# Paced loads, reordered weight sums and a split last product in a fused attention and MLP kernel on one Trainium2 core

## The chip, the cores and the metric

The kernel runs on one core of one Trainium2 chip. The metric is the device time of one execution in microseconds (us); the median of several executions is given, with the lowest and the highest. A profile is taken from one more execution, whose own time is given beside it. The engines are called by their short names: PE (matrix products; PEld is its loading of weights), DVE and ACT (elementwise work), POOL (which here issues most loads), SP (which issues stores and transposes).

## The reference

Two stages follow each other. The first is linear attention with a decay `lam` per head, over 4 batches, 8 heads, 768 positions and 64 channels. In blocks of positions, with a running state S of 64 x 64 per head:

```
out_block = ((q k^T) * decay_mask) v  +  (q * lam^(pos+1)) S
S         = lam^block * S  +  (k * lam^(block-1-pos))^T v
```

The second takes the attention output as x, 3072 tokens by 512, and is a two-layer network:

```
h = x @ w_in                       # 512 -> 2048
g = h * tanh(log(1 + exp(h)))      # Mish
out = g @ w_out                    # 2048 -> 512
```

Inputs and the output are float32; the kernel computes its products in float16 with float32 sums.

## The kernel before

**Tiles and groups.** The sequence is cut into chunks of 128 positions. Chunk i = 4 n + b is piece n of batch b, and the four chunks of one n make a group of 512 tokens; there are six groups, n = 0 to 5. The network of group n runs on PE while attention of the next groups is worked in between its units.

**Loads.** POOL issues nearly all loads (they turn float32 into float16 on the way): K, Q and V of each chunk (`load_k`, `load_q`, `load_v`, L61 to L78), the weight w_in in six tiles whose column bounds stand in `cuts` (L82), and w_out in four tiles of 512 rows (L98). In program order the first group's chunks come first, then w_in, w_out, then the second group's chunks 4 to 7. The list `ahead` (L314) holds the twelve loads of the third group, chunks 8 to 11: K and Q of each chunk in turn, then the four V. The loop over the first group's units takes two of them after each unit from 25 to 29 (L645), and the last two go out after the first unit of group 1 (L684). Later groups' loads go out one by one behind `pace()` (L395), a copy of one element on POOL that waits for the newest entry of the list `mark`, an output of Mish or of a copy on ACT.

**Attention.** For chunks 0 to 7 the `look_...` functions are used: `look_t` (L204) transposes K and Q on PE, evicts K's transpose on ACT (pkT) and Q's on DVE (pqT); `look_s` (L226) makes the scores, masked on DVE; `look_kv` the state's increment; `look_o` the output. `scale_k` (L262) makes the decayed K (ktil), on DVE but for chunks 6 and 7, which POOL makes. From chunk 8 on `turn` (L269) scales K and lets two DMA transposes, issued on SP, make qraw and kraw; pairs of chunks are then worked by `pair_s` (scores, L338), `pair_o` and `pair_a`. In group 1 the turns of chunks 8, 9, 10 and 11 are issued after units 0, 1, 4 and 7, and `pair_s` of chunks 8 and 9 stands after unit 11.

**The network.** Units 0 to 15 are w_in products with Mish on ACT behind each. The second product is done with seven products instead of eight on halves of g and w_out: P1, P5, P6, P2, P7, P3, P4 (`fast_unit`, L550). They need sums of quarters of w_out, `tsum` 0 to 3, made once on DVE by `weight_sum(i, s)` (L452), in two halves s; half s = 1 of every sum but 0 needs the last w_out tile. They also need sums of quarters of g, `gsum` (`token_sum`, L465). P6 reads sum 1, P5 sum 0, P7 sum 2 and P4 sum 3. In group 0 the units are numbered 16, 17 (P1), 18, 19 (P5), 20 to 23 (P6, P2, P6, P2, in halves of the inner dimension), 24, 25 (P7), 26, 27 (P3), 28, 29 (P4). A loop (L625 to L649) runs these units and puts in between what the dictionaries name: weight sums after units 14, 15, 18 and 20, ktil of chunk 4 after unit 22, `look_t(4)` after 23, `look_s(4)` after 24, and so on.

**What follows a product.** `after(n, step)` (L526) copies a finished PSUM bank into the next product's bank or into an SBUF tile, and issues the store. P1's bank x is copied to z, to which P6 adds; P6's z is copied to y, P7 and then P4 add to z, P3 adds to y. P7 and P3 get P5's product added on DVE (`plus`, L518). The last P4 of the last group (L561) is done in three pieces: block 0 whole, block 1 in two halves of 128 columns; each is copied by ACT from bank z and stored from SP.

**Order.** The program is scheduled by hand: each engine and each queue works in the order in which the instructions are written. Waits are put in by data, PSUM bank and buffer.

Of the kernel before, what the change touches and what calls it, by code (L numbers as in the profile page):

```python
# [20 lines left out]
def kernel(  # L21
# [10 lines left out]
    nc = tc.nc  # L32
# [46 lines left out]

    WS = 4  # L80

    cuts = (0, 128, 256, 512, 1024, 1536, DF)  # L82
    win = [const.tile([128, NKC, b_ - a_], F16, name=f"win{a_}") for a_, b_ in zip(cuts, cuts[1:])]

    def w_in(ni, kc):
# [309 lines left out]
    def pace():  # L395
        nc.gpsimd.tensor_copy(paced, mark[-1])  # L396
# [125 lines left out]
        store(n, r, c, o, nc.sync)  # L522

    p5 = {}

    def after(n, step):  # L526

        if step == "P1":
            nc.scalar.activation(places(n, "z"), bank[n, "x"], AF.Copy)
        elif step == "P2":  # L530
            o = work.tile([128, 2, HN], F32, name="osum", tag="osb", bufs=4)
            nc.scalar.activation(o, bank[n, "x"], AF.Copy)
            mark.append(o[0:1, 0, 0:1])
            store(n, 0, 0, o, nc.scalar)
        elif step == "P6":
            nc.scalar.activation(places(n, "y"), bank[n, "z"], AF.Copy)
        elif step == "P5":
            p5[n] = work.tile([128, 2, HN], F32, name="p5", tag="p5", bufs=1)
            nc.scalar.activation(p5[n], bank[n, "w"], AF.Copy)
            mark.append(p5[n][0:1, 0, 0:1])  # L540
        elif step == "P7":
            plus(n, 1, 1, "z")
        elif step == "P3":
            plus(n, 0, 1, "y")
        elif step == "P4":
            o = work.tile([128, 2, HN], F32, name="osum", tag="osb", bufs=4)
            nc.scalar.activation(o, bank[n, "z"], AF.Copy)  # L547
            store(n, 1, 0, o, nc.scalar)

    def fast_unit(n, step, blk, part=None):  # L550

        key, lhs, rhs = {
            "P1": lambda: ("x", g_quarter(n, 0, 0), w_part(0, 0)),
            "P2": lambda: ("x", g_quarter(n, 0, 1), w_part(1, 0)),
            "P6": lambda: ("z", g_sum(n, 1), w_sum(1)),
            "P5": lambda: ("w", g_sum(n, 0), w_sum(0)),
            "P7": lambda: ("z", g_sum(n, 2), w_sum(2)),
            "P3": lambda: ("y", g_sum(n, 3), w_part(1, 1)),
            "P4": lambda: ("z", g_quarter(n, 1, 1), w_sum(3)),
        }[step]()  # L560
        if n == NG - 1 and step == "P4":  # L561
            for lo, hi in ((0, HN),) if blk == 0 else ((0, HN // 2), (HN // 2, HN)):
                product(n, key, lhs, rhs, False, blk, None, lo, hi)
                o = work.tile([128, 1, HN], F32, name="osum", tag="osb", bufs=4)
                nc.scalar.activation(o[:, 0, lo:hi], bank[n, "z"][:, blk, lo:hi], AF.Copy)  # L565
                store(n, 1, 0, o[:, :, lo:hi], nc.sync, blk, lo, hi)
            return
        for b in range(2) if blk is None else (blk,):
            product(n, key, lhs, rhs, step in ("P1", "P5"), b, part)
        if blk != 0 and part != 0:  # L570
            after(n, step)

    nc.scalar.activation(lbh, lnb, AF.Exp, scale=float(C))
    nc.scalar.activation(lk, lnb, AF.Exp, scale=ek)
# [48 lines left out]
    units += [(fast_unit, (0, step, blk)) for step in ("P7", "P3", "P4") for blk in range(2)]  # L623
    sums = {3: ((2, 0),), 7: ((2, 1),), 11: ((0, 0), (1, 0), (3, 0)), 15: ((0, 1), (1, 1)), 16: ((3, 1),)}
    for u, (fn, args) in enumerate(units):  # L625
        fn(*args)
        if 8 <= u < 8 + NVB - B:
            nc.vector.memset(vz[u - 8 + B][:, :, D : 2 * D], 0.0)
        elif u == 13:
            nc.vector.tensor_scalar(out=maskT, in0=rel, scalar1=0.0, scalar2=None, op0=ALU.is_ge)  # L630
        for i, s in {14: ((0, 0),), 15: ((0, 1),), 18: ((1, 0), (2, 0), (3, 0)),
                     20: ((1, 1), (2, 1), (3, 1))}.get(u, ()):
            weight_sum(i, s)
        for i, part in sums.get(u, ()):
            token_sum(0, i, part)
        if u == 22:
            scale_k(4)
        then = [f(i, "po" if i == 5 else "ph") if f is look_kv else f(i) for f, i in visit.get(u, ())]
        if u == 23:
            scale_k(5)  # L640
            scale_k(6)
        for f in then:
            if f:
                f()
        if u >= 25:  # L645
            for _ in range(2):
                ahead.pop(0)()
        if u == 26:
            scale_k(7)  # L649
    next_state(1, 0)  # L650

    for n in range(1, NG):
        r, s, t = Pair(), Pair(), Pair()
        r.n, r.bs, s.n, s.bs, t.n, t.bs = n, (2, 3), n + 1, (0, 1), n + 1, (2, 3)
        visit = {}
        if n > 1:
            visit[0] = pair_o, last
        if 1 < n < NG - 1:
            visit[5] = pair_a, r
        if n < NG - 1:  # L660
            visit[9 if n > 1 else 11] = pair_s, s
            visit[16] = pair_o, s
            visit[26] = pair_s, t
        if n < NG - 2:
            visit[21] = pair_a, s
        last = t
        turns = {23: (n + 2) * B, 25: (n + 2) * B + 1}
        turns.update({1: 9, 4: 10, 7: 11} if n == 1 else {3: (n + 1) * B + 2, 6: (n + 1) * B + 3})
        units = [(mm1_duo, (n, g, lo, lo + GT // 2)) for lo in (0, GT // 2) for g in range(NKI // 2)]
        steps = ("P1", "P5", "P6", "P2", "P7", "P3", "P4")  # L670
        units += [(fast_unit, (n, step, blk)) for step in steps for blk in range(2)]
        later = []
        if n < NG - 2:
            later = [(lambda f=f, i=(n + 2) * B + b: f(i)) for f, b in (
                (load_k, 0), (load_q, 0), (load_k, 1), (load_q, 1), (load_k, 2), (load_q, 2),
                (load_v, 0), (load_v, 1), (load_k, 3), (load_q, 3), (load_v, 2), (load_v, 3))]
        sums = {9: ((2, 0),), 11: ((2, 1),), NKI - 3: ((0, 0), (1, 0)), NKI - 1: ((0, 1), (1, 1)),
                NKI + 4: ((3, 0),), NKI + 5: ((3, 1),)}
        for u, (fn, args) in enumerate(units):
            fn(*args)  # L680
            if n == 1 and u == 0:
                turn(8)
                look_s(7)
                while ahead:  # L684
                    ahead.pop(0)()
            if n == 1 and u == 2:
                f = look_kv(7)
                look_o(7)
                f()
                next_state(1, 1)  # L690
            if later and (8 <= u < 16 or u in (17, 19, 21, 23)):
                pace()
                later.pop(0)()
            for i, part in sums.get(u, ()):
                token_sum(n, i, part)
            if turns.get(u, NG * B) < NG * B:
                turn(turns[u])
            if u in visit:
                f, s_ = visit[u]
                s_.spare = ("po", "po") if u < NKI - 1 else ("pS", "pk") if f is pair_a else ("ph", "po")  # L700
                f(s_)
# [30 lines left out]
```

## Time and profile before

| | us |
|---|---|
| median of 3 executions | 204.13 |
| lowest and highest | 204.04 and 205.29 |
| the profiled execution, its own time | 205.4 |
| span of the profiled execution, first to last instruction | 203.6 |
| chain that ended last: share of PE | 71% |
| chain that ended last: share of DMA | 17% |

In the profile, a row of the timeline or of the chain gives start, duration and what was done, with the idle time of the engine ahead of it and what ended that in square brackets. L434 is line 434 of the kernel. A row of the table of waits gives who waited for whom, the sum, the number of times and the longest. A row of a group of instructions gives line, engine, operation, output and inputs with shapes, the count, then busy time and the mean of one in ns, then idle time before them. All times are in us from the start of the span.

### The profile page before, as it was taken

Reading aid. Unit: us, or ns where it says so; the run is one execution under the profiler, and the core shown is the slowest. Engines: PE = TensorE matmul, PEld = TensorE weight load, DVE = VectorE, ACT = ScalarE, POOL = GpSimd, SP = SyncE. Lnnn points to the kernel's source line nnn. Section 1 sums busy time; section 2 is a strip of 40 time slices with the busy share of each in tenths; the row PEclk is TensorE's granted clock in tenths of the full one; section 3 lists DMA queues with packets and bytes.
Section 4 is the critical chain, followed back from the end, with each engine's and each line's share of the span. In section 5 each row is a group of like instructions: output and inputs, shape, how many; then the busy total and the mean of one; then the engine's idle time right before and its main releaser. Section 6 shows DMA issues by size and latency. Waiting matters only on the chain.

```text
span 203.6 us, 5043 instructions
## 1 busy us (share of the span) xinstructions
PE 192.7 (95%) x2080; PEld 160.3 (79%) x2080; DVE 131.1 (64%) x248; ACT 91.9 (45%) x160; POOL 81.0 (40%) x124
## 2 busy tenths in 40 slices
PE   7869999899997999999999999999999999999992
PEld 3554447678885998998998998998988988988881
DVE  7897169689943878847878757878557817215420
ACT  5784664233664431365531455420565330666311
POOL 7997333589907583005992006982000000000000
PEclk9999999999999999999999999999999999999999
DMA  9999999999999999956999989999981023500033
GB/s 132 140 156 183 201 206 199 153 193 183 177 148 129 154 119 193 225 123 76 103 127 182 221 131 88 96 98 187 276 110 29 0 55 103 159 0 0 3 103 103
DMA packets 112985, 26.81 MB, mean 132 GB/s; under 512 B 102594, under 2 KB 112962, under 8 KB 112962
## 3 DMA queue, kind: packets, MB, share of 16 engines
q0 software_dynamic: 78080, 13.37, 91.4%
q1 hardware_dynamic: 30848, 9.97, 29.1%
q10 hardware_dynamic: 4034, 3.15, 5.0%
q8 instruction: 16, 0.26, 0.5%
q14 instruction: 7, 0.06, 0.1%
HBM read 27.26 MB, written 6.29 MB: 165 GB/s over the span
## 4 chain that ended last, share of the span: by engine, by line
PE 71%; DMA 17%; POOL 5%; DVE 3%; ACT 1%; issue 1%; ACTq 0%; POOLq 0%
PE ph L434 29%; PE z L494 15%; DMA wout<-in_moe_w_out_dram 10%; PE x L494 9%; PE y L494 5%; DMA kraw<-ktil 4%; PE w L494 4%; DMA win<-in_moe_w_in_dram 3%; PE pS L349 2%; PE pO L376 2%; POOL vz L78 2%; POOL kn L67 1%; PE pv L328 1%; POOL qn L75 1%; PE pO L357 1%
## 5 line engine op out<-in xcount | busy, mean ns | idle before, releaser
L434 PE MATMUL ph<-xt,win 128*128 128x256 f16 x640 | 73.0, 273 | 0.0
L434 PEld LDWEIGHTS <-win 128*128 128x128 f16 x640 | 61.6, 98 | 7.5 <-issue 0.3
L441 ACT ACTIVATE hsg<-ph 128x512 f16<-128x512 f32 x80 | 47.8, 597 | 30.7 <-PE ph L434 30.7
L494 PEld LDWEIGHTS <-gsum 128*128 128x128 f16 x384 | 36.9, 98 | 6.0 <-issue 1.2
L480 DVE TENSOR_TENSOR gsum<-hsg 128x1024 f16<-128x1024 f16 x24 | 16.6, 691 | 29.6 <-ACT hsg L441 22.4
L494 PEld LDWEIGHTS <-hsg 128*128 128x128 f16 x296 | 27.9, 98 | 4.4 <-issue 1.1
L494 PE MATMUL z<-tsum,gsum 128*128 128x256 f16 x192 | 23.3, 273 | 1.0 <-DVE tsum L461 1.0
L494 PE MATMUL x<-wout,hsg 128*128 128x256 f16 x192 | 23.7, 273 | 0.0
L67 POOL DMA_DIRECT2D kn<-in_k_dram x23 | 20.6, 894 | 7.5 <-DMA win<-in_moe_w_in_dram 2.6
L75 POOL DMA_DIRECT2D qn<-in_q_dram x23 | 20.4, 889 | 5.9 <-DMA wout<-in_moe_w_out_dram 4.3
L78 POOL DMA_DIRECT2D vz<-in_v_dram x24 | 21.2, 891 | 4.0 <-DMA wout<-in_moe_w_out_dram 1.7
L396 POOL COPY paced<-hsg 1x1 f16<-1x1 f16 x27 | 8.7, 324 | 35.1 <-ACT hsg L441 35.1
L365 DVE TENSOR_TENSOR sb<-pS,maskT 128x512 f16<-128x512 f32 x32 | 19.9, 684 | 1.9 <-PE pS L349 1.6
L288 DVE TENSOR_TENSOR raw<-pv,state 64x256 f32<-64x256 f32 x24 | 10.1, 422 | 12.8 <-PE pv L328 12.5
L265 DVE TENSOR_TENSOR ktil<-kn,lk 128x512 f16<-128x512 f16 (+1 forms) x22 | 14.9, 684 | 0.0
L405 PE MATMUL ph<-xt,win 128*128 128x512 f16 x64 | 14.2, 379 | 0.3 <-DMA win<-in_moe_w_in_dram 0.3
L384 DVE TENSOR_TENSOR xtok<-pO,lqt 128x256 f16<-128x256 f32 x32 | 11.3, 416 | 3.9 <-PE pO L376 3.9
L547 ACT ACTIVATE osum<-z 128x512 f32<-128x512 f32 x5 | 3.0, 597 | 23.6 <-PE z L494 23.6
L494 PE MATMUL z<-tsum,hsg 128*128 128x256 f16 (+1 forms) x104 | 12.0, 264 | 0.8 <-ACT osum L565 0.8
L405 PEld LDWEIGHTS <-win 128*128 128x128 f16 x64 | 6.2, 98 | 7.9 <-DMA win<-in_moe_w_in_dram 0.8
L494 PE MATMUL y<-wout,gsum 128*128 128x256 f16 x96 | 12.3, 273 | 0.0
L417 ACT ACTIVATE hsg<-ph 128x512 f16<-128x512 f32 x16 | 9.6, 597 | 6.0 <-PE ph L405 6.0
(90 smaller groups left out, 197.0 us busy)
## 6 DMA issues: line engine op xcount, KB each, us to landing
vz<-in_v_dram POOLq DMA_DIRECT2D x24, 128.0 KB, 6.3
out_dram<-osum SPq DMA_DIRECT2D x12, 256.0 KB, 4.2
kn<-in_k_dram POOLq DMA_DIRECT2D x23, 128.0 KB, 5.2
qn<-in_q_dram POOLq DMA_DIRECT2D x23, 128.0 KB, 5.2
out_dram<-osum ACTq DMA_DIRECT2D x11, 256.0 KB, 4.0
wout<-in_moe_w_out_dram POOLq DMA_DIRECT2D x4, 512.0 KB, 16.6
win<-in_moe_w_in_dram POOLq DMA_DIRECT2D x3, 512.0 KB, 10.2
kn<-in_k_dram SPq DMA_DIRECT2D x1, 256.0 KB, 3.3
```

The lines of the kernel that those rows point to most:

```text
L67: nc.gpsimd.dma_start(out=kn[i], in_=chunk_rows(k, i))
L75: nc.gpsimd.dma_start(out=qn[i], in_=chunk_rows(q, i))
L78: nc.gpsimd.dma_start(out=vz[i % NVB][:, :, 0:D], in_=chunk_rows(v, i))
L265: (nc.gpsimd if B + 1 < i < 2 * B else nc.vector).tensor_tensor(out=t, in0=kn[i], in1=bc(lk, 2, D), op=ALU.mult)
L288: nc.vector.tensor_tensor(out=raw[rs, b % 2, j0 : j0 + nj, :], in0=pv[rs, :, rs], in1=olds(rs), op=ALU.add)
L365: nc.vector.tensor_tensor(out=s.sb[m][t], in0=sc[m][t], in1=bc(maskT, 1, JP), op=ALU.mult)
L384: nc.vector.tensor_tensor(out=xtok[m][:, :, t, :], in0=s.pO[t][:, m], in1=bc(lt[:, :, t], 2, D), op=ALU.mult)
L405: nc.tensor.matmul(ph_t[ni][:, lo:hi], w_in(ni, kc), xt[n][:, kc, lo:hi], start=(kc == 0), stop=(kc == NKC - 1),)
L434: nc.tensor.matmul(t[:, m, lo - half * h : hi - half * h], w_in(ni, kc), xt[n][:, kc, lo:hi], start=(m == 0 and kc == 0), stop=(kc == NKC ...
L441: nc.scalar.activation(hsg[n][:, 2 * g : 2 * g + 2, half * h : half * h + h], t, AF.Mish)
L480: nc.vector.tensor_tensor(out=gsum[n, i][:, ks, :], in0=a, in1=b, op=op)
L494: nc.tensor.matmul(places(n, key)[:, blk, lo:hi], lhs(kk, blk), rhs(kk, lo, hi), start=(fresh and kk == 0 and blk == 0), stop=(kk == HK - ...
```

## The change

Five things are edited.

1. `cuts`: the first two w_in tiles, columns 0 to 127 and 128 to 255, become one tile of 256 columns, so there are five w_in loads.
2. `weight_sum` in group 0: half (1,0) stays after unit 18, (1,1) moves up to unit 19, and (2,0), (2,1), (3,0), (3,1) all come after unit 20. Before, (1,0), (2,0), (3,0) came after unit 18 and (1,1), (2,1), (3,1) after unit 20.
3. In group 0, what follows P2 (unit 23: a copy on ACT and a store from ACT's queue) and P7 (unit 25: a sum on DVE and a store) is put off behind the attention work of the same unit.
4. The third group's loads: six go out after units 25, 26 and 27 of group 0, as before, and the other six (K and Q of chunk 11 and the four V) behind `pace()` after units 0, 1, 2 (two of them), 3 and 4 of group 1. Before, four of these went out after units 28 and 29 of group 0 and two after unit 0 of group 1, without a wait.
5. The last group: after P7, ACT copies bank z to an SBUF tile `u3`. The three pieces of the last P4 are then summed afresh in three other PSUM banks (those of the tags pS, pk and pO), and DVE adds `u3` to each on the way out, where ACT copied before.

```
-    cuts = (0, 128, 256, 512, 1024, 1536, DF)
+    cuts = (0, 256, 512, 1024, 1536, DF)
...
+    u3 = []
...
         elif step == "P7":
+            if n == NG - 1:
+                u3.append(work.tile([128, 2, HN], F32, name="u3", tag="osb", bufs=4))
+                nc.scalar.activation(u3[0], bank[n, "z"], AF.Copy)
             plus(n, 1, 1, "z")
...
-    def fast_unit(n, step, blk, part=None):
+    def fast_unit(n, step, blk, part=None, then=None):
...
         if n == NG - 1 and step == "P4":
-            for lo, hi in ((0, HN),) if blk == 0 else ((0, HN // 2), (HN // 2, HN)):
-                product(n, key, lhs, rhs, False, blk, None, lo, hi)
-                o = work.tile([128, 1, HN], F32, name="osum", tag="osb", bufs=4)
-                nc.scalar.activation(o[:, 0, lo:hi], bank[n, "z"][:, blk, lo:hi], AF.Copy)
-                store(n, 1, 0, o[:, :, lo:hi], nc.sync, blk, lo, hi)
+            for lo, hi, g in ((0, HN, "pS"),) if blk == 0 else ((0, HN // 2, "pk"), (HN // 2, HN, "pO")):
+                fin = ps.tile([128, hi - lo], F32, name="fin", tag=g)
+                for kk in range(HK):
+                    nc.tensor.matmul(fin, lhs(kk, blk), rhs(kk, lo, hi),
+                                     start=(kk == 0), stop=(kk == HK - 1))
+                o = work.tile([128, 1, hi - lo], F32, name="osum", tag=f"end{g}", bufs=1)
+                nc.vector.tensor_tensor(out=o[:, 0], in0=fin, in1=u3[0][:, blk, lo:hi], op=ALU.add)
+                store(n, 1, 0, o, nc.sync, blk, lo, hi)
             return
...
         if blk != 0 and part != 0:
-            after(n, step)
+            if then is None:
+                after(n, step)
+            else:
+                then.append(lambda: after(n, step))
...
     for u, (fn, args) in enumerate(units):
-        fn(*args)
+        put_off = []
+        fn(*args, **({"then": put_off} if u in (23, 25) else {}))
...
-        for i, s in {14: ((0, 0),), 15: ((0, 1),), 18: ((1, 0), (2, 0), (3, 0)),
-                     20: ((1, 1), (2, 1), (3, 1))}.get(u, ()):
+        for i, s in {14: ((0, 0),), 15: ((0, 1),), 18: ((1, 0),), 19: ((1, 1),),
+                     20: ((2, 0), (2, 1), (3, 0), (3, 1))}.get(u, ()):
             weight_sum(i, s)
...
-        for f in then:
+        for f in put_off + then:
             if f:
                 f()
-        if u >= 25:
+        if u in (25, 26, 27):
             for _ in range(2):
                 ahead.pop(0)()
...
             if n == 1 and u == 0:
                 turn(8)
                 look_s(7)
-                while ahead:
-                    ahead.pop(0)()
...
+            for _ in range({0: 1, 1: 1, 2: 2, 3: 1, 4: 1}.get(u, 0) if n == 1 else 0):
+                pace()
+                ahead.pop(0)()
```

## The prediction

> **What bounds the kernel now.** I read the page first. Its busy row and its row of granted clock:
>
> ```profile
> PE 192.7 (95%) x2080; PEld 160.3 (79%) x2080; DVE 131.1 (64%) x248; ACT 91.9 (45%) x160; POOL 81.0 (40%) x124
> PEclk9999999999999999999999999999999999999999
> ```
>
> TensorE is busy for 95% of the span at full clock, and the change removes no matmul. Only PE's idle time and the tail behind its last matmul can be won. Second I asked who waited for whom, and kept PE's rows that the diff touches:
>
> ```profile
> PE pS L349 <- DMA kraw<-ktil: 1.5, 1, 1.5
> PE z L494 <- DVE tsum L461: 1.0, 1, 1.0
> PE z L494 <- ACT osum L565: 0.8, 2, 0.5
> ```
>
> Three parts of the change answer to these three rows, 3.3 us in all; the fourth, the copies put off, answers to a wait of 0.36 that stands in the next fence. Third I read the timeline around each.
>
> **The weight sums and the copy put off (34 to 42 us).** The timeline of DVE, PE and ACT:
>
> ```profile
> 35.73 0.68 DVE L461 TENSOR_TENSOR tsum<-wout,tsum 128x1024 f16<-128x1024 f16 x1
> 37.43 0.69 DVE L461 TENSOR_TENSOR tsum<-wout,tsum 128x1024 f16<-128x1024 f16 x1 [1.01 <-DMA wout<-in_moe_w_out_dram]
> ...
> 38.17 1.03 PE L494 MATMUL z<-tsum,gsum 128*128 128x256 f16 x8 [0.98 <-DVE tsum L461]
> ...
> 39.04 1.04 PE L494 MATMUL x<-wout,hsg 128*128 128x256 f16 x8
> 39.24 0.68 DVE L265 TENSOR_TENSOR ktil<-kn,lk 128x512 f16<-128x512 f16 x1
> 39.98 0.40 PE L211 MATMUL pk<-ident,ktil 128*128 128x128 f16 x4
> 40.12 0.60 ACT L532 ACTIVATE osum<-x 128x512 f32<-128x512 f32 x1 [0.23 <-PE x L494]
> 40.64 0.69 DVE L219 TENSOR_TENSOR pqT<-pq,lq 128x512 f16<-128x512 f16 x1 [0.72 <-PE pq L211]
> 40.74 0.39 ACTq L516 DMA_DIRECT2D out_dram<-osum  x1
> 41.19 0.60 ACT L223 ACTIVATE pkT<-pk 128x512 f16<-128x512 f16 x1 [0.47 <-ACT osum L532]
> 41.84 0.40 PE L234 MATMUL pS<-pqT,pkT 64*128 64x128 f16 x8 [0.36 <-ACT pkT L223]
> ```
>
> At 37.43 the last w_out tile lands and DVE makes the second half of sum 1. The second half of P6 starts at 38.17, and DVE makes two more sums between 37.43 and 39.24, where ktil of chunk 4 follows. The first halves of sums 2 and 3 had been made earlier, the last at 35.73, in time that DVE would have spent waiting. The change sends (1,1) directly behind (1,0), and all four halves of sums 2 and 3 behind it. DVE works in order, so (2,0) and (3,0) now stand behind an instruction that waits for w_out. Four sums follow that landing where two did.
>
> If (1,1) starts at time T, ktil of chunk 4 starts five steps later. A step is (39.24 - 37.43) / 3 = 0.60 us, so that is T + 3.02. PE's transpose follows 39.98 - 39.24 = 0.74 behind it, at T + 3.76. PE itself would be free sooner: P6's half starts at T + 0.74, and two halves of 0.87 (39.04 - 38.17) bring it to T + 2.48. PE would thus have a new wait of 1.28 us.
>
> What is T? The change merges the first two w_in tiles (columns 0 to 127 and 128 to 255), which stand ahead of w_out in POOL's queue. That saves one POOL issue; DMA transfers are queued behind POOL throughout there, so it can save DMA time only if larger pieces go faster. Two stretches in which the loads had small and large pieces:
>
> ```profile
> 20.00:22.00 2.00, 1.73 (x9) 0.65 (x8) 0.33 (x1) 1.19 (x2) 0.71 (x2) 1.00 1.24 206
> 38.00:40.00 2.00, 1.83 (x17) 1.48 (x17) 1.93 (x4) 0.58 (x1) 2.00 (x3) 1.00 2.43 155
> ```
>
> This is the table of windows; its last column is GB/s written. From 38 to 40 chunk loads run (128-byte rows of fp16), from 20 to 22 w_in (1 KB rows). Two 128 KB tiles take 0.262 MB / 155 = 1.69 us at the slow rate, one 256 KB tile 1.27 at the fast one. The bounds of the gain are 0 and 0.42 us. The true sizes are 256 and 512 bytes, one doubling out of three between those rows, so I take a third, 0.15: T = 37.28.
>
> The Trainium skill, page DMA: Bandwidth & Descriptors, section Specifications, says that line rate needs 512 B or more, with a read-modify-write below that. By that rule the merged tile would take half of 1.69 and T would fall by 0.85; that is rival 1.
>
> The first unit of the first group now needs the 256-column tile, which can land about when the second small one did. The chain of waits has that tile, and the timeline the next wait of PE for w_in:
>
> ```profile
> 11.31 6.10 DMA win<-in_moe_w_in_dram
> 21.27 10.53 PE L405 MATMUL ph<-xt,win 128*128 128x512 f16 x48 [0.27 <-DMA win<-in_moe_w_in_dram]
> ```
>
> PE has 0.27 us of idle time ahead of 21.27, so a unit that starts a tenth later than now costs 0. Without that cover it would cost the tenth.
>
> Now look_s(4), 41.84 before. The transpose at T + 3.76 = 41.04 is 1.06 later than 39.98. pqT follows in the same step: 40.64 + 1.06 = 41.70, done 42.39, PE at 42.44. The copy put off is P2's: ACT no longer runs osum (0.60) and its store issue (0.39) ahead of pkT. pkT can go at 41.04 + 0.40 = 41.44, done 42.04, before pqT. So putting the copy off would be worth up to 0.45 by itself (41.84 against pqT's end 41.33 plus 0.05), but here it is hidden behind DVE. P7's sum, also put off, moves behind pqT of chunk 5; PE meets no wait there before, so 0. Sum of this stage: 42.44 - 41.84 = **+0.60 us**. Its bounds are -0.45 (w_out early enough that neither sums nor copy bind) and +0.75 (T unchanged).
>
> **The paced loads (50 to 66 us).** POOL, ACT, DVE and PE, and a later pair of the same kind at 80 us that waits for nothing:
>
> ```profile
> 51.99 3.53 POOL L78 DMA_DIRECT2D vz<-in_v_dram  x4
> 52.72 0.60 ACT L441 ACTIVATE hsg<-ph 128x512 f16<-128x512 f32 x1
> ...
> 57.46 0.60 ACT L441 ACTIVATE hsg<-ph 128x512 f16<-128x512 f32 x1 [0.28 <-PE ph L434]
> ...
> 61.61 0.18 POOL L396 COPY paced<-hsg 1x1 f16<-1x1 f16 x1 [6.09 <-ACT hsg L441]
> 62.45 0.69 DVE L480 TENSOR_TENSOR gsum<-hsg 128x1024 f16<-128x1024 f16 x1 [4.31 <-ACT hsg L441]
> 63.47 0.40 PE L349 MATMUL pS<-qraw,kraw 64*128 64x128 f16 x8
> 65.36 0.40 PE L349 MATMUL pS<-qraw,kraw 64*128 64x128 f16 x8 [1.49 <-DMA kraw<-ktil]
> 65.92 3.67 PE L434 MATMUL ph<-xt,win 128*128 128x256 f16 x32
> 80.04 0.62 PE L349 MATMUL pS<-qraw,kraw 64*128 64x128 f16 x16
> 80.83 1.05 PE L494 MATMUL y<-wout,gsum 128*128 128x256 f16 x8
> ```
>
> Unhindered, PE needs 80.83 - 80.04 = 0.79 us from the first pS to the next matmul; here it took 65.92 - 63.47 = 2.45. The stall is worth **1.66 us**. It ends when kraw of chunk 9 lands, 8.97 us after its issue at 56.34. Over all groups this transpose takes:
>
> ```profile
> DMA to landing us min/median/max: 2.4/4.8/9.0
> 56.34 8.97 DMA kraw<-ktil
> ```
>
> The first row is the tile view of kraw, the second the chain of waits, in which this is the last DMA. Six loads are in flight with it: POOL issues the four V of the third group from 51.99 on, 0.88 each, and K and Q of chunk 11 just before, from about 50.2. The change issues them after waits on Mish of units 0 to 4: the first ends at 52.72 + 0.60 and the fifth at 57.46 + 0.60, both 0.60 later by the stage above, so 53.92 and 58.66. With a copy and some 0.3 us ahead of each, the six issues run from about 54.2 to 59.4.
>
> What is queued behind POOL's waits is only these loads; the next pace copy comes at 61.61, behind 6.09 idle. Chunk 11's K comes four us later, so ktil of 11 stands on DVE until about 60, and behind it is the token sum of 62.45: 2 us of cover. If it came later than 63, P5 would wait for its token sums. Chunk 11's transposes wait on SP for its Q; they are read at 80.04. V is first read in pair_o, behind the matmuls that start at 65.92. I cost these at 0.
>
> SP's kraw issue follows DVE and PE, so it moves to 56.94, and PE reaches that pS at 63.47 + 0.60 + 0.23 (half a pS group) = 64.30. The transpose has 7.4 us. With the median of 4.8 it lands at 61.7 and the stall is gone: **-1.66**. Bounds: the minimum 2.4 gives the same, the maximum 9.0 leaves 65.9, worth -0.05. I take the median's side, because the six loads that made the maximum are not yet, or only just, in the queue when it is issued.
>
> **The last product (197 us on).**
>
> ```profile
> 197.56 1.04 PE L494 MATMUL z<-tsum,hsg 128*128 128x256 f16 x8
> 197.76 0.69 DVE L521 TENSOR_TENSOR osum<-y,p 128x512 f32<-128x512 f32 x1 [1.00 <-PE y L494]
> 199.07 0.61 PE L494 MATMUL z<-tsum,hsg 128*128 128x128 f16 x8 [0.47 <-ACT osum L565]
> 200.04 0.61 PE L494 MATMUL z<-tsum,hsg 128*128 128x128 f16 x8 [0.36 <-ACT osum L565]
> ...
> 200.99 0.33 SPq L516 DMA_DIRECT2D out_dram<-osum  x1
> L384 DVE TENSOR_TENSOR xtok<-pO,lqt 128x256 f16<-128x256 f32 x32 | 11.3, 416 | 3.9 <-PE pO L376 3.9
> L365 DVE TENSOR_TENSOR sb<-pS,maskT 128x512 f16<-128x512 f32 x32 | 19.9, 684 | 1.9 <-PE pS L349 1.6
> ```
>
> Each third waits for ACT's read of the one before, as all share a bank. In three banks PE runs through: eight matmuls of 256 columns at 0.109 (0.87), then eight of 128 at 0.056 ((0.61 - 0.22) / 7). The second third starts at 198.43, the last at 198.87 and ends at 199.48. DVE's adds take 0.42 for 256 columns (row L384) and, with its slope to row L365, 0.28 for 128. DVE is free at 198.45; the adds end at 199.06, 199.36 and 199.80. SP issues the three stores from 199.08 some 0.42 apart (0.33 and a gap), the last at 199.92 instead of 200.99: **-1.07**. Bounds: -0.8 (PE's two waits alone) to -1.17 (PE's whole gain, SP not binding). The added ACT copy of z (0.60) runs under P3; if P7's add has to wait for it, DVE ends that at 197.4, before 197.76. No price.
>
> **Sum.** +0.60 - 1.66 - 1.07 = -2.13 us. The profiled execution has 203.6 us of span and 205.4 in its own time; the sum moves it to 201.5 and 203.3. The median shown is 204.13, 1.27 below that execution; I take the difference over: **202.0 us**, 1.0% faster.
>
> **The rivals.**
> 1. *w_out lands early.* If 512-byte rows cost half as much per byte as 256-byte rows, the merged tile saves 0.85 us, T = 36.58, and look_s(4) starts at 41.74: -0.10 instead of +0.60, total -2.83, 201.3 us. Against it, 155 and 206 GB/s differ by a third only, over three doublings. With T below 36 the sum reaches -0.45 - 1.66 - 1.07 = -3.2 and 200.9. Chance 0.17. This is the time that the rule of the page's section Specifications would give; the trace's two windows bear it out only in direction.
> 2. *The pacing does nothing.* The transposes stay as slow as before, 9.0 us, PE still waits till 65.9, and the total is +0.60 - 0.05 - 1.07 = -0.52, 203.6 us. For it: the same six loads still go out between 54 and 60 us, and kraw of 9 goes out at 56.94, among them. Against it: the median of 4.8, most of it from groups whose loads are paced already. Chance 0.12. The Trainium skill, page DMA: Bandwidth & Descriptors, section Queues, rings and completion order, says that a DMA engine takes turns between the queues for which it has work; by that rule one waiting load slows a transpose as much as six do, which is this rival.
> 3. *Slower than before*: the paced loads come to stand exactly before kraw of 9. The loads issued with the four V took
>
> ```profile
> DMA to landing us min/median/max: 7.3/9.0/10.9
> ```
>
> With 10.9 the transpose lands at 67.8, PE stands 3.5 us, and the total is +0.60 + 1.9 - 1.07 = +1.4, 205.6 us. It decides from a landing at 66.4 on (9.5 us). Chance 0.04.
>
> **How the numbers follow.** The forecast has 0.67, rivals 0.17, 0.12 and 0.04. About 1% is what a measurement of this kernel can tell from no change, and the edge is 202.09, at the forecast itself; so I halve its 0.67, and with rival 1 faster by over 1% has 0.50. Within 1% has 0.48 (the other half, rival 2, most of rival 3), slower 0.02. The range runs from the far end of rival 1 to rival 2, 200.9 to 203.6: these are the bounds of the two costs that no row settles, w_out's landing and the transposes' time. It leaves out rival 3. The likeliest case alone, with its bounds of 0.15 and 0.27 and the transposes landing in time, spans 201.5 to 202.5.
>
> **What would show it.** In the changed profile DVE's ktil of chunk 4 stands five sums' steps behind w_out and PE waits there about 1.3 us; the 0.98 wait for tsum is about 0.8; no wait of pkT for osum; no wait for kraw at 64; no wait of P4 for osum and the last store some 1.1 us nearer to P3's end. The prediction is wrong if w_out lands before 36.6, if kraw of 9 lands after 64.3, or if P6's first half waits for (1,1), now ahead of it in DVE.

## The result and the profile after

| | before | after |
|---|---|---|
| median | 203.93 us (22 executions) | 202.82 us (22 executions) |
| lowest and highest | 202.89 and 205.29 | 201.58 and 203.66 |
| ratio | | 0.9941, 95% interval 0.9922 to 0.9959 |
| the profiled execution, its own time (span) | 205.4 (203.6) | 202.06 (200.3) |

The change gains 1.2 us, 0.6% (0.8 to 1.6 us); 2.1 us had been forecast. A second measurement, beside 11 executions of the kernel before, gave 0.9915 (0.9890 to 0.9939), 1.7 us. The ratios leave out executions more than 1.5% above the fastest of their kernel, which the medians further down include, and the profile of the kernel after without the pacing is of such an execution (206.69 us).

The two profiled executions differ by 3.3 us, three times as much as the medians: the one of before was slower than all 22 of its kernel, the one of after is the third fastest of its 22. So a difference of these two profiles is not yet an effect of the change, and each stage has to be measured from its own start. The busy row of after:

```profile
PE 192.1 (96%) x2080; PEld 160.7 (80%) x2080; DVE 131.8 (66%) x251; ACT 91.7 (46%) x158; POOL 81.6 (41%) x129
```

PE does the same 2080 matmuls in the same time; what has changed is idle time. From the table of waits, the rows of this kernel that are new:

```profile
DVE osum L521 <- ACT u L545: 6.1, 1, 6.1
DVE ktil L265 <- DMA kn<-in_k_dram: 1.9, 1, 1.9
PE pk L211 <- DVE ktil L265: 0.9, 1, 0.9
DVE tsum L461 <- DMA wout<-in_moe_w_out_dram: 0.9, 1, 0.9
PE ph L434 <- DMA xt<-xtok: 0.2, 1, 0.2
```

PE's rows for kraw (1.5), tsum (1.0) and osum (0.8) are gone; in their place PE waits 0.9 us for ktil of chunk 4. The last row is a short wait late in the span. (`pk` is the transpose of K in `look_t(4)`, `u` the copy of z on ACT, the tile that the diff calls `u3`.)

**The weight sums.** The timeline from 35 to 41 us:

```profile
35.62 0.69 DVE L461 TENSOR_TENSOR tsum<-wout,tsum 128x1024 f16<-128x1024 f16 x1 [0.88 <-DMA wout<-in_moe_w_out_dram]
36.23 1.29 DVE L461 TENSOR_TENSOR tsum<-wout,wout 128x1024 f16<-128x1024 f16 x2
36.55 1.04 PE L494 MATMUL z<-tsum,gsum 128*128 128x256 f16 x8
37.44 1.29 DVE L461 TENSOR_TENSOR tsum<-wout,tsum 128x1024 f16<-128x1024 f16 x2
38.64 0.69 DVE L265 TENSOR_TENSOR ktil<-kn,lk 128x512 f16<-128x512 f16 x1
39.38 0.40 PE L211 MATMUL pk<-ident,ktil 128*128 128x128 f16 x4 [0.92 <-DVE ktil L265]
39.82 0.60 ACT L223 ACTIVATE pkT<-pk 128x512 f16<-128x512 f16 x1 [1.55 <-PE pk L211]
40.04 0.69 DVE L219 TENSOR_TENSOR pqT<-pq,lq 128x512 f16<-128x512 f16 x1 [0.72 <-PE pq L211]
40.31 0.59 ACT L533 ACTIVATE osum<-x 128x512 f32<-128x512 f32 x1
40.81 0.40 PE L234 MATMUL pS<-pqT,pkT 64*128 64x128 f16 x8
```

DVE waits for w_out at 35.62 with sums 2 and 3 still to make; the four halves run behind it from 36.23 to 38.64 (two rows of two), and only then comes ktil. T, the start of (1,1) in the prediction, is 35.62, 0.02 behind the landing of w_out at 35.60; the transpose starts at T + 3.76 and `look_s(4)` at T + 5.19. The copy put off (ACT, 40.31) now runs behind pkT, whose eviction ends at 40.42; pqT ends at 40.73, so it is DVE that PE waits for.

**The paced loads.** POOL, SP, DVE and PE from 52 to 63 us:

```profile
52.63 0.87 POOL L67 DMA_DIRECT2D kn<-in_k_dram  x1
55.13 2.31 SPq L274 DMA_TRANSPOSE kraw<-ktil  x1
55.14 0.87 POOL L78 DMA_DIRECT2D vz<-in_v_dram  x1
58.37 0.70 DVE L265 TENSOR_TENSOR ktil<-kn,lk 128x512 f16<-128x512 f16 x1 [1.85 <-DMA kn<-in_k_dram]
58.47 0.87 POOL L78 DMA_DIRECT2D vz<-in_v_dram  x1
61.42 0.69 DVE L480 TENSOR_TENSOR gsum<-hsg 128x1024 f16<-128x1024 f16 x1 [2.35 <-ACT hsg L441]
62.44 0.62 PE L349 MATMUL pS<-qraw,kraw 64*128 64x128 f16 x16
63.23 3.67 PE L434 MATMUL ph<-xt,win 128*128 128x256 f16 x32
```

The six issues run from 52.63 (K of chunk 11) to 58.47 (the last V). All sixteen pS matmuls of chunks 8 and 9 stand in one row, 0.79 us from its start to the next matmul. Chunk 11's K is late, as forecast: its ktil waits 1.85 us on DVE and ends at 59.07, ahead of the token sum of 61.42. The two kraw transposes issued at 55.13 and 58.85 took, by the tile view of kraw in that window:

```profile
DMA to landing us min/median/max: 6.5/6.7/6.8
```

**The end.** The timeline from 194 us, then SP's last issue:

```profile
194.10 0.69 DVE L521 TENSOR_TENSOR osum<-z,p 128x512 f32<-128x512 f32 x1 [6.11 <-ACT u L545]
195.01 1.93 PE L569 MATMUL fin<-tsum,hsg 128*128 128x256 f16 x24
195.22 0.69 DVE L521 TENSOR_TENSOR osum<-y,p 128x512 f32<-128x512 f32 x1 [0.43 <-PE y L494]
196.09 0.74 DVE L572 TENSOR_TENSOR osum<-fin,u 128x256 f32<-128x256 f32 x2 [0.18 <-PE fin L569]
196.98 0.29 DVE L572 TENSOR_TENSOR osum<-fin,u 128x128 f32<-128x128 f32 x1 [0.15 <-PE fin L569]
```

```profile
197.48 0.40 SPq L516 DMA_DIRECT2D out_dram<-osum  x1
```

The 24 matmuls run without a break, in 1.93 us. From the start of P4 to the last store's issue it is 197.48 - 195.01 = 2.47 us, before 200.99 - 197.56 = 3.43. P7's sum (194.10) waited for the new ACT copy of z, and DVE was free again at 194.79, 0.43 us before P3's product was ready: no price.

### The profile page after: what moved, and what is told of

It reads as the page before. It is cut to its first block, busy times and chain, and to the rows that moved or that the text cites. A ratio compares the mean times of both kernels' runs of the same rounds, so it can differ in the third digit from the quotient of the medians.

```text
span 200.3 us, 5050 instructions
## 1 busy us (share of the span) xinstructions
PE 192.1 (96%) x2080; PEld 160.7 (80%) x2080; DVE 131.8 (66%) x251; ACT 91.7 (46%) x158; POOL 81.6 (41%) x129
## 4 chain that ended last, share of the span: by engine, by line
PE 75%; DMA 12%; POOL 8%; DVE 3%; issue 1%; SPq 0%; POOLq 0%
PE ph L434 32%; PE z L494 14%; DMA wout<-in_moe_w_out_dram 9%; PE x L494 9%; PE y L494 6%; PE w L494 4%; PE pS L349 2%; DMA xt<-xtok 2%; POOL win L93 2%; PE pO L376 2%; POOL vz L78 2%; DVE tsum L461 2%; POOL kn L67 1%; PE pv L328 1%; POOL qn L75 1%; POOL wout L100 1%
## 5 line engine op out<-in xcount | busy, mean ns | idle before, releaser
L494 PEld LDWEIGHTS <-hsg 128*128 128x128 f16 x272 | 26.1, 98 | 3.2
L396 POOL COPY paced<-hsg 1x1 f16<-1x1 f16 x33 | 10.4, 315 | 31.7 <-ACT hsg L441 31.6
L521 DVE TENSOR_TENSOR osum<-z,p 128x512 f32<-128x512 f32 x6 | 4.1, 690 | 12.9 <-issue 6.8
```

Of the source, the lines that this page charges most:

```text
L494: nc.tensor.matmul(places(n, key)[:, blk, lo:hi], lhs(kk, blk), rhs(kk, lo, hi), start=(fresh and kk == 0 and blk == 0), stop=(kk == HK - ...
```

## The experiments

The parts of the diff are undone one by one in the kernel after, and three of them done one by one in the kernel before. All ratios are to the kernel before, timed on the same chip in the same series; 0.1% is 0.2 us. Undoing the merged tile and the copies put off was done in the kernel after alone.

| kernel | median us | ratio, 95% interval |
|---|---|---|
| after, old order of the weight sums | 201.60 | 0.9884 (0.9840 to 0.9929) |
| after, loads not paced | 204.47 | 1.0008 (0.9973 to 1.0043) |
| after, old last product | 203.08 | 0.9954 (0.9927 to 0.9982) |
| after, two small w_in tiles | 202.72 | 0.9944 (0.9915 to 0.9972) |
| after, copies not put off | 202.52 | 0.9917 (0.9891 to 0.9943) |
| after, sums recombined | 201.81 | 0.9885 (0.9856 to 0.9914) |
| the same with the old last product | 202.62 | 0.9897 (0.9874 to 0.9920) |
| before, new last product only | 202.53 | 0.9919 (0.9891 to 0.9948) |
| before, new order of the sums only | 204.60 | 1.0019 (0.9998 to 1.0041) |
| before, paced loads only | 202.43 | 0.9912 (0.9885 to 0.9939) |
| after, a second time | 202.71 | 0.9915 (0.9890 to 0.9939) |

### After with the old order of the weight sums

```
-        for i, s in {14: ((0, 0),), 15: ((0, 1),), 18: ((1, 0),), 19: ((1, 1),),
-                     20: ((2, 0), (2, 1), (3, 0), (3, 1))}.get(u, ()):
+        for i, s in {14: ((0, 0),), 15: ((0, 1),), 18: ((1, 0), (2, 0), (3, 0)),
+                     20: ((1, 1), (2, 1), (3, 1))}.get(u, ()):
```

> The changed kernel with only the weight sums back in their old order ((1,0), (2,0), (3,0) after unit 18; (1,1), (2,1), (3,1) after unit 20). Theory 1 (the prediction's: the new order puts four sums between w_out's landing and ktil of chunk 4, and PE stood 0.92 us there in the profile after): faster than the changed kernel by 0.6 to 1.0 us, so a ratio to before of about 0.990, and no wait of PE for ktil of chunk 4. Theory 2 (the new order is what lets P6 run on without a wait): slower than the changed kernel by up to 0.9 us, ratio about 0.998, with a wait of P6 for its sum.

Measured: 0.9884, against 0.9941 and 0.9915 with the new order: 1.2 and 0.6 us faster, each uncertain by 1.0. The direction is that of theory 1, and the 0.6 to 1.0 that it gave fits both; the times alone don't settle it, as the intervals overlap. PE's table of waits has no row for ktil of chunk 4. In its profile w_out lands at 37.02, and

```profile
38.85 0.68 DVE L265 TENSOR_TENSOR ktil<-kn,lk 128x512 f16<-128x512 f16 x1
39.59 0.40 PE L211 MATMUL pk<-ident,ktil 128*128 128x128 f16 x4
40.03 0.60 ACT L223 ACTIVATE pkT<-pk 128x512 f16<-128x512 f16 x1 [0.53 <-PE pk L211]
41.02 0.40 PE L234 MATMUL pS<-pqT,pkT 64*128 64x128 f16 x8
```

`look_s(4)` starts 4.00 us behind that landing: 1.2 us less than the 5.21 after it in the kernel after, and 0.43 less than in the kernel before (37.41 to 41.84), because here the copy is put off and pkT no longer waits for it. So the copy put off is worth the 0.45 that the prediction gave it, but only in the old order.

### After with the last six loads not paced

```
-            for _ in range({0: 1, 1: 1, 2: 2, 3: 1, 4: 1}.get(u, 0) if n == 1 else 0):
-                pace()
-                ahead.pop(0)()
```

The loads go out after units 28 and 29 of group 0 and unit 0 of group 1, as in the kernel before.

> The changed kernel with the third group's last six loads issued as before, without pacing. Theory 1: the wait for kraw of chunk 9 comes back, 1.5 us or more, ratio to before about 1.002. Theory 2 (the transposes are late only in some executions, and the pacing gives little on the whole): within 0.5 us of the changed kernel, ratio 0.994 to 0.997.

Measured: 1.0008 against 0.9941 for the kernel after: without the pacing 1.4 us are lost ((1.0008 - 0.9941) x 204.1; the two intervals allow 0.6 to 2.2). PE's wait for kraw in its profile, and the kraw transpose of chunk 9, the one issued between 54 and 60 us:

```profile
PE pS L349 <- DMA kraw<-ktil: 2.5, 2, 2.2
```

```profile
DMA to landing us min/median/max: 9.2/9.2/9.2
```

9.2 us to landing, against 6.8 for chunk 9 in the kernel after. The stall is back, 2.2 us for chunk 9 and 0.3 for chunk 8. Its size is not read from this execution, which took 2.2 us more than the median of its kernel; that of the kernel before had 1.5.

### After with the old last product

```
-            for lo, hi, g in ((0, HN, "pS"),) if blk == 0 else ((0, HN // 2, "pk"), (HN // 2, HN, "pO")):
+            for lo, hi in ((0, HN),) if blk == 0 else ((0, HN // 2), (HN // 2, HN)):
...
-                nc.vector.tensor_tensor(out=o[:, 0], in0=fin, in1=u3[0][:, blk, lo:hi], op=ALU.add)
+                nc.scalar.activation(o[:, 0, lo:hi], bank[n, "z"][:, blk, lo:hi], AF.Copy)
```

> The changed kernel with the last product as before (one bank, ACT copies). Theory 1: the last store is issued 0.96 us later after the start of the last P4 (2.47 us in the profile after, 3.43 before), time up by 0.9 to 1.1 us, ratio to before about 0.999. Theory 2 (the tail of the stores hides it): up by less than 0.4 us.

Measured: 0.9954, that is 0.3 us slower than after in the medians, with an uncertainty of 0.7 (both intervals): too wide to size the part. It is theory 2's figure, with theory 1's 0.9 just inside the uncertainty. The trace does size it, since this stage starts with PE and waits for no load. P4 starts at 194.57 and the last store goes out at 198.00, 3.43 us later, to the digit that of the kernel before; PE waits 0.47 and 0.36 for ACT again.

This profile also shows when the new order of the sums costs little. w_out landed at 35.48, the earliest of all, and PE came to the last half of P2 only at 38.12:

```profile
39.26 0.40 PE L211 MATMUL pk<-ident,ktil 128*128 128x128 f16 x4
```

The transpose starts 1.14 us behind that half. In the recombined kernel further down, where PE does not wait there, it is 0.88 (38.01 to 38.89). So the new order costs PE 0.3 us here, against 1.1 in the kernel after (37.43 to 39.38) and 1.3 in the five other profiles that have it.

### After with the two small w_in tiles

```
-    cuts = (0, 256, 512, 1024, 1536, DF)
+    cuts = (0, 128, 256, 512, 1024, 1536, DF)
```

> The changed kernel with the two w_in tiles of 128 columns instead of one of 256. Theory 1 (the prediction: the merge is worth 0 to 0.42 us of DMA time): w_out lands 0.1 to 0.4 us later, time up by 0 to 0.4. Theory 2 (the merge is what made w_out land 1.8 us earlier in the profile after): w_out lands at 36.5 to 37.4 instead of 35.6, time up by 0.8 us or more.

Measured: 0.9944, the same as the kernel after. The last w_out tile landed at 36.15 us in this profile. Over all thirteen profiles (before, after, eleven experiments) it landed between 35.48 and 37.41: on average at 36.25 in the eight with the merged tile and at 36.63 in the five with two tiles, a difference of 0.4 with an uncertainty of 0.7. So the 1.8 us of theory 2 are not the merge's, and a few tenths, theory 1, are neither shown nor excluded.

### After with the sums recombined

The first halves stand early, as in the old order, (1,1) and then ktil of chunk 4 directly behind w_out, and the other second halves behind ktil.

```
-        for i, s in {14: ((0, 0),), 15: ((0, 1),), 18: ((1, 0),), 19: ((1, 1),),
-                     20: ((2, 0), (2, 1), (3, 0), (3, 1))}.get(u, ()):
+        for i, s in {14: ((0, 0),), 15: ((0, 1),), 18: ((1, 0), (2, 0), (3, 0)),
+                     20: ((1, 1),)}.get(u, ()):
...
+        if u == 20:
+            scale_k(4)
         if u == 22:
-            scale_k(4)
+            weight_sum(2, 1)
+            weight_sum(3, 1)
```

> The changed kernel with the first halves (2,0) and (3,0) back behind (1,0), then (1,1), ktil of chunk 4 straight behind it, and (2,1) and (3,1) after that. Theory 1 (only what DVE does between w_out's landing and ktil counts): no wait of PE for ktil, look_s(4) 3.9 us after (1,1) starts (5.2 in the changed kernel, 4.0 with the old order of the sums), so 1.2 us faster than the changed kernel and within 0.3 of the run with the old order. Theory 2 (PE then meets the next limit, P7 waiting for (2,1)): a wait of P7 for tsum, and less than 0.6 us gained.

Measured: 0.9885 (0.9856 to 0.9914), 2.4 us below before. It is faster than the first measurement of the kernel after beyond the noise, and 0.6 us below the second, within it. It equals the old order with the rest of the change (0.9884): moving ktil ahead as well gains nothing that shows. The timeline:

```profile
36.40 0.69 DVE L461 TENSOR_TENSOR tsum<-wout,tsum 128x1024 f16<-128x1024 f16 x1 [0.46 <-DMA wout<-in_moe_w_out_dram]
37.14 1.03 PE L494 MATMUL z<-tsum,gsum 128*128 128x256 f16 x8 [0.43 <-DVE tsum L461]
37.25 0.69 DVE L265 TENSOR_TENSOR ktil<-kn,lk 128x512 f16<-128x512 f16 x1 [0.16 <-DMA kn<-in_k_dram]
38.89 0.39 PE L211 MATMUL pk<-ident,ktil 128*128 128x128 f16 x4
40.30 0.40 PE L234 MATMUL pS<-pqT,pkT 64*128 64x128 f16 x8
```

ktil is ready at 37.94, a microsecond before PE's transpose at 38.89: now PE itself is the bound, and `look_s(4)` starts 3.93 us behind w_out, as theory 1 had it.

### Before with the new last product only

```
+            if n == NG - 1:
+                u3.append(work.tile([128, 2, HN], F32, name="u3", tag="osb", bufs=4))
+                nc.scalar.activation(u3[0], bank[n, "z"], AF.Copy)
...
+            for lo, hi, g in ((0, HN, "pS"),) if blk == 0 else ((0, HN // 2, "pk"), (HN // 2, HN, "pO")):
```

> The kernel before with only the last product in three banks. Theory 1: from the start of P3's last matmul group to the last store 2.57 us instead of 3.54, time down by 0.85 to 1.0 us, ratio 0.9955. Theory 2 (as the run of the changed kernel with the old end suggests, which was only 0.26 us slower): down by 0.3 us, ratio 0.9985.

Measured: 0.9919, 1.6 us (1.1 to 2.2). That is more than the stage can hold: in its profile it is 5.31 us from the last y matmul to the end of the span where before has 6.18, so the stage gives 0.87. The wait for kraw happens to be 1.0 us in this execution instead of 1.5. What gave the rest of the 1.6 us isn't shown.

### After with the copies not put off

```
-        fn(*args, **({"then": put_off} if u in (23, 25) else {}))
+        fn(*args, **({"then": put_off} if u in () else {}))
```

> The changed kernel without putting off what follows P2 and P7. Theory 1 (DVE's sums hide it): within 0.2 us of the changed kernel, PE's wait before look_t(4) unchanged. Theory 2: pkT waits for the copy, up by 0.4 us.

Measured: 0.9917, between the two measurements of the kernel after (0.9941 and 0.9915). w_out lands at 36.02 and `look_s(4)` starts at 41.23, 5.21 behind: the same to the digit.

```profile
38.73 0.60 ACT L533 ACTIVATE osum<-x 128x512 f32<-128x512 f32 x1 [0.23 <-PE x L494]
39.36 0.39 ACTq L516 DMA_DIRECT2D out_dram<-osum  x1
39.80 0.40 PE L211 MATMUL pk<-ident,ktil 128*128 128x128 f16 x4 [1.11 <-DVE ktil L265]
40.24 0.60 ACT L223 ACTIVATE pkT<-pk 128x512 f16<-128x512 f16 x1 [0.91 <-PE pk L211]
41.23 0.40 PE L234 MATMUL pS<-pqT,pkT 64*128 64x128 f16 x8
```

The copy and its store end at 39.75, while PE waits for ktil: the new order of the sums made the gap in which the copy is free.

### Before with the new order of the sums only

The diff is the first one of this section, the other way round, in the kernel before.

> The kernel before with only the new order of the weight sums. Theory 1: look_s(4) 5.2 us after (1,1) starts instead of 4.43, PE waits about 1.2 us for ktil of chunk 4, time up by 0.75 us, ratio 1.0037. Theory 2 (the order helps P6): faster than before by up to 0.9 us.

Measured: 1.0019 (0.9998 to 1.0041), 0.4 us slower, with no change just inside the interval; theory 1's 1.0037 is inside it too, and the gain of theory 2 is all but excluded. `look_s(4)` starts 5.21 us behind w_out, 4.43 in the kernel before. Its waits of PE:

```profile
PE pS L349 <- DMA kraw<-ktil: 1.6, 1, 1.6
PE pk L211 <- DVE ktil L265: 1.1, 1, 1.1
PE z L494 <- ACT osum L565: 0.8, 2, 0.5
```

### Before with the paced loads only

The last six loads of `ahead` behind `pace()` as in the change, nothing else.

> The kernel before with the pacing of the last six loads alone; weight sums, copies, w_in tiles and last product as before. Theory (the pacing is worth the 1.35 us that the changed kernel lost without it): the stall of PE for kraw of chunk 9 goes, 202.6 to 203.2 us beside a before of 204.0, ratio about 0.994. Rival A (the stall that the pacing removes is worth the 1.66 of the profile shown first or more, 2.5 as in the run without the pacing): ratio 0.992 or less. Rival B (the changed kernel lost that time in the run without the pacing only because the later start of chunk 4 put its loads closer to the transposes): ratio above 0.997, and the wait for kraw in the kernel before is under 1 us in the median.

Measured: 0.9912, 1.8 us (1.2 to 2.3). PE's table of waits has no row for kraw any more, and the transpose of chunk 9 lands in 6.9 us. Rival B, that the pacing only helps the kernel after, is out. This profile also shows the old order of the sums with an early w_out (landed at 35.70):

```profile
37.71 0.68 DVE L265 TENSOR_TENSOR ktil<-kn,lk 128x512 f16<-128x512 f16 x1
38.45 0.40 PE L211 MATMUL pk<-ident,ktil 128*128 128x128 f16 x4
39.66 0.60 ACT L223 ACTIVATE pkT<-pk 128x512 f16<-128x512 f16 x1 [0.47 <-ACT osum L532]
40.31 0.40 PE L234 MATMUL pS<-pqT,pkT 64*128 64x128 f16 x8 [0.36 <-ACT pkT L223]
```

`look_s(4)` at 40.31, with w_out 0.10 later than in the profile of after, where it is 40.81. The old order no longer waits for w_out here, and between these two executions the new one costs 0.5 us.

### Recombined sums with the old last product, and after once more

> The recombined order of the weight sums, with pacing, but with the old last product. Theory (the end is worth 0.85 us of the span whatever stands before it): 0.85 slower than the recombined kernel, which was at 0.9885, so ratio about 0.9925; last store issued 3.5 us behind the start of the last P3 block and not 2.6. Rival (the store's own landing evens the end out, as the 0.27 of the changed kernel with the old end hinted): within 0.3 us of the recombined kernel, ratio 0.990 or less.

> The changed kernel once more, on the chip of the two runs beside it. Theory (parts add up): -1.35 for the pacing, -0.85 for the end and +0.8 to +1.2 for the weight sums give -1.0 to -1.4 us, ratio 0.993 to 0.995, slower than the old-end kernel with the recombined sums by some 0.3 us. Rival (the weight sums cost nothing in the median, since w_out lands when it likes): ratio 0.990 or less.

Measured: 0.9897 for the first, 0.2 us above the recombined kernel's 0.9885 with an uncertainty of 0.8. That is the rival's ratio and not the theory's 0.9925. In the trace the theory holds: the store went out 3.54 us behind the last y matmul, against 2.57 with the new end. So by the times the end is worth 0.3 and 0.2 us with the other parts and 1.6 alone, by the traces 0.8 to 0.9 wherever it was read; why the times scatter so isn't shown. The kernel after had 0.9915, between its theory and its rival. Its profile lost a microsecond that no part of the change touches, at 150 us:

```profile
149.90 1.91 PE L434 MATMUL ph<-xt,win 128*128 128x256 f16 x16 [0.60 <-DMA xt<-xtok]
```

Such a wait, 0.6 and 0.8 us, stands in two of the thirteen profiles (this one and the copies not put off); one of 0.2 us stands in this one, in that of the kernel after and in that of the recombined sums with the old end. All four have the paced loads, and none of the four profiles without them has it. Whether the change favours it isn't settled.

### The stages side by side

Since w_out's landing and whole executions differ by a microsecond or more, the stages of each profile are measured from their own start (us):

| profile | last w_out lands | `look_s(4)` behind it | PE's wait for kraw | last y matmul to end of span |
|---|---|---|---|---|
| before | 37.41 | 4.43 | 1.5 | 6.18 |
| before, new sums | 36.73 | 5.21 | 1.6 | 6.17 |
| before, new end | 37.18 | 4.44 | 1.0 | 5.31 |
| before, paced | 35.70 | 4.61 | none | 6.18 |
| after | 35.60 | 5.21 | none | 5.35 |
| after again | 36.45 | 5.21 | none | 5.33 |
| after, old sums | 37.02 | 4.00 | none | 5.35 |
| after, not paced | 36.10 | 5.21 | 2.5 | 5.33 |
| after, old end | 35.48 | 5.20 | none | 6.22 |
| after, recombined | 36.37 | 3.93 | none | 5.35 |

The stages agree with the parts wherever a part is present, whatever stands beside it; the last column, from the start of the last y matmul, is 6.2 with the old end and 5.3 with the new one in all ten. The second column says how long the stage takes from the landing on; what PE loses by it also depends on how early w_out lands, as the profile with the old end showed.

A second way to the sizes uses the times alone. Each of the twelve ratios (the eleven above and the result) less one, times 204.1 us, is taken as a sum of the parts that its kernel holds, weighted by its interval. The fit gives +0.7 for the new order of the sums, -1.5 for the pacing, -0.7 for the end, each with about 0.35 by the intervals; as the twelve scatter around the fit 1.6 times as much as their intervals allow, about 0.5 is the honest uncertainty. The recombined order gives -0.4, of the same size as its uncertainty. The parts add up to -1.5, between the two measurements of the kernel after (-1.2 and -1.7).

## Why the prediction was right, and where its sizes were off

| step | forecast | stage in the traces | fit of the times |
|---|---|---|---|
| order of the sums, copy put off | +0.60 | +0.78 (5.21 - 4.43), less where w_out lands early | +0.7 |
| paced loads | -1.66 | -1.0 to -1.6, execution by execution | -1.5 |
| last product | -1.07 | -0.83 (6.18 - 5.35) | -0.7 |
| sum | -2.13 | | -1.5 |

The direction and the three mechanisms were right; the gain came out at 1.2 us, 0.9 less than forecast. All three terms were too favourable. By the fit they make up 0.6 of the 0.9, but each is uncertain by 0.5, so the times do not say which was furthest off. The prediction took 1% for the least that a measurement can tell from no change; here 0.6% was told.

**The sums.** Right, down to the digits: the prediction put the transpose at T + 3.76 and `look_s(4)` at 42.44 for T = 37.28, that is T + 5.16; the profile has T + 3.76 and T + 5.19. A first half of a sum that DVE could make while it waited for a load was moved behind that wait, and DVE's backlog then held PE. What failed is T: it was read from one execution, as if it were a property of the kernel. It varies by 1.9 us between executions, and the prediction's own test ("wrong if w_out lands before 36.6") came out true in the profile of after (35.60) without rival 1's being right: before with the paced loads, which has the two small tiles, landed at 35.70. With w_out so early PE lost 1.1 us at the transpose and not the forecast 1.3, which five profiles with a later landing show, and the wait of 0.8 that was forecast for the second half of P6 did not come. Of the 0.78 that the stage costs from its landing on, the prediction took off 0.15 for the merged tile; the remaining 0.03 is rounding of the steps.

**The merged tile** (rival 1). Not shown. The times with and without it are equal within 0.7 us, and the forecast 0.15 is too small to be seen here. The Trainium skill, page DMA: Bandwidth & Descriptors, section Specifications, says that line rate needs 512 B or more, with a read-modify-write below that, and gives there no factor; the half on which 0.85 rested was the prediction's own reading. The landings (0.4, uncertain by 0.7) neither show nor exclude it.

**The copy put off.** Right on both counts: 0.43 alone, nothing in the new order.

**The pacing.** The mechanism is shown from both sides, by the kernel after without it and the kernel before with it; rival 2, no effect, is refuted. The transpose of chunk 9 took 8.3 to 9.0 us in three profiles without the pacing (before, new end, new sums) and 6.4 to 7.1 in all nine with it. So the loads that are under way when it is issued do slow it. From the Trainium skill, page DMA: Bandwidth & Descriptors, section Queues, rings and completion order, rival 2 drew that one waiting load slows a transpose as much as six; that is not borne out here, while the rule itself, that a DMA engine takes turns between its queues, no run here shows. But the median of 4.8 on which the step rested was also wrong for this place. It was taken over all groups, most of them with less beside them: 11 of the 15 kraw transposes in the profile before were issued with three or fewer of POOL's loads in flight. Here six loads were in flight in the profile before when the transpose of chunk 9 was issued (they landed from 57.21 to 65.51); in the profile after two were, and the four V were issued while it was under way (55.14 to 58.47). It was issued at 55.13 and landed at 61.94, and PE came to it at 62.67: 0.7 us of margin and not 2.6. The size of the gain is that of the stall, which is 1.0, 1.5 and 1.6 us in those three profiles; the forecast took the whole of one of them. Each of the three is of an execution slower than the median of its kernel, so the stall of a median execution is not known from a trace.

**The last product.** Right in kind, 0.2 us too large in size. PE ran through and the last store went out 0.96 us nearer to P4's start. The prediction had 0.42 us from one store issue to the next and gave 199.92 - 197.56 = 2.36 from P4's start; it took 2.47. The stores stood 0.44 and 0.50 apart. The rest, 0.12, is the last store's own time: 1.55 us from issue to landing before, 1.67 after.

**The reference point.** The sum was worked out against an execution of 205.4 us and then carried to the median as a difference. Its stall (1.5) lies within what other executions without the pacing show, so this did little harm there; but its landing of w_out, the latest of thirteen, went into T.

Rival 3, slower than before, did not come: in the nine profiles with the pacing no transpose of chunks 9 and 10 took more than 7.4 us.

## What to carry to other kernels

An instruction on an in-order engine that waits for a load should have behind it only what depends on that load; work that is ready goes ahead of it, or the engine has a backlog when the load lands. When one execution's landing times go into a forecast, ask first how far they vary from one execution to the next, and forecast in terms that do not contain them. Two profiles that differ by more than the medians have to be compared stage by stage, each from its own start.

## What the runs showed of the hardware

- The time at which the last of four 512 KB loads landed differed by 1.9 us (35.48 to 37.41) between executions, with no pattern by kernel that stands out of the scatter; stages without loads repeated within 0.02 us (5.20 or 5.21 in seven profiles; 3.43 twice).
- The same DMA transpose took 8.3 to 9.0 us to land, in three profiles, with six loads of 128 KB issued ahead of it and still in flight, and 6.8 and 6.9 us (kernel after, kernel before with the paced loads) with two of them ahead and four issued during its flight; the smallest time in the kernel before was 2.4, with none ahead.
- The last three stores issued on SP stood 0.44 and 0.50 us apart in the kernel after (196.54, 196.98, 197.48), the last taking 0.40 us to issue, though its sum had ended on DVE at 197.27; in the kernel before, where each waited for ACT, they stood 0.97 and 0.98 apart and the last took 0.33.
